# A tile's weight decoding in halves, with its last operation on GpSimd

## The chip, the core and the metric

The kernel runs on one core of a Trainium2 chip. The core has a matrix engine (TensorE, PE in the profile; its weight loads are PEld), a vector engine (VectorE, DVE), an engine for functions of one operand (ScalarE, ACT), a programmable engine (GpSimd, POOL) and one that issues transfers (SyncE, SP). Each engine works through its own instructions in a fixed order, and semaphores make it wait for the others. The metric is the time of one execution on the device in microseconds (us), the median of several runs.

## The reference

The reference computes one attention layer with a memory term and two feed-forward layers behind it, on 2304 rows of 512 numbers:

```python
def _attn_ref(q, k, v, M_prev, z_prev, beta):        # B, H, S, D = 4, 8, 576, 64
    scores = scale * q @ k.T; scores = where(causal, -1e9, scores)
    a = exp(scores - scores.max(-1)); a /= a.sum(-1) + 1e-09
    local = a @ v
    q_p = phi(q)                                      # where(x > 0, x, exp(x) - 1) + 1
    mem_out = (q_p @ M_prev) / (q_p @ z_prev + 1e-06)
    g = sigmoid(beta)
    return g * mem_out + (1 - g) * local

def _moe_ref(x, w_in, w_out):                         # 2304 x 512, 512 x 2048, 2048 x 512
    h = x @ w_in
    return (h * sigmoid(1.702 * h)) @ w_out

def _moe2_ref(x, w_in, w_out):
    h = x @ w_in
    return (h * clip(h + 3, 0, 6) / 6) @ w_out
```

The second layer works on the first one's result. Inputs and outputs are float32.

## The kernel before

The rows are cut into six tiles of 384 (TILES): tiles 0, 1, 3 and 4 are the first 384 rows of a batch, tiles 2 and 5 the last 192 rows of two batches. The hidden width of 2048 is cut into NF = 16 steps f of 128. For a layer, a tile and a step, moe() does the up-projection h (four matmuls, one for each 128 of the 512 inputs, lines 344 to 351), the gate (lines 280 to 301: a function on ScalarE, line 285, then a product on VectorE, line 287, which reads h once more and writes g), and the down-projection y (four accumulating matmuls, lines 317 to 321). In the first layer's first tile the matmuls take float32 operands as they are (lines 346 and 317); everywhere else weights and activations are split in two parts and each product is done as three. Through the first layer h has one buffer, so that the next up-projection can write it only when VectorE has read the last one.

The attention of the later tiles is computed while the earlier ones are in the first layer. Its work for each pair of heads (scores s, line 428; softmax: minimum, exponential, sum and reciprocal, lines 490 to 499; scaling of the probabilities p by GpSimd, line 503; transposes t, line 443; memory term; weighted sum o) is handed out between the matmuls by pump(), and the scheduler described below puts some of it still earlier. The form differs for the last 192 rows of a batch (index 2 and 5): with them come the scalings of p4 and p5, 512 and 64 columns. In the second half of the first tile such work, for the tile with index 2, is what stands between the matmuls.

The weights come from memory as raw 64-bit words seen as pairs of 32-bit words lo and hi, and are decoded in place by conv_w(), one step f at a time: VectorE shifts lo (line 190) and joins it with hi (195); ScalarE brings hi towards a sign (199) while the sign bit of lo is cleared, on ScalarE (201) or on VectorE (203) as ABS says: for the first layer's steps above PRE = 2 on ScalarE where f is even; ScalarE takes the sign of hi (205); VectorE limits lo and multiplies with the sign (210). A step's tile holds the weights of both projections, [128, 2, 512] pairs: index 0 is for the up-, index 1 for the down-projection. For the first layer line 210 writes the result over the raw words, and the first tile's matmuls read it there. The decoding of the 16 steps of the first layer runs during the attention that comes first (steps 0 to 2) and during the first tile.

The kernel is written as generators that hand out instructions in small steps (Chains); what stands in an engine's queue in the end is decided by a scheduler that replays the whole program with its own costs and puts ready instructions in order. A change of one operation can so move others on all engines.

## Time and profile before

| | us |
|---|---|
| median of 3 runs | 1046.57 |
| lowest, highest | 1045.54, 1046.84 |
| profiled execution | 1045.53 |
| its span, first to last instruction | 1043.4 |
| TensorE busy | 1011.2 (97%) |
| VectorE busy | 496.6 (48%) |
| ScalarE busy | 533.1 (51%) |
| GpSimd busy | 295.2 (28%) |

The span is what the views of the trace cover; the rest of an execution's time lies around it. Busy shares are means over the whole program; in the first 260 us, while attention and decoding run, VectorE and ScalarE are busier than later. A wait in a view is the time in which an engine stood idle just before an instruction, with the instruction that let it go.

### The profile page before, as it was taken

What the parts mean: (1) busy time and instruction counts of PE and PEld (TensorE: products, weight loads), DVE (VectorE), ACT (ScalarE), POOL (GpSimd) and SP (SyncE); (2) the same over time, 40 slices, a digit from 0 to 9 for tenths busy, and PEclk for the clock granted to TensorE, in tenths of its full rate; (3) what the DMA queues carried; (4) which work ended last, traced back from release to release, by engine and by line L of the source; (5) the groups of instructions that cost most, each with busy time, mean ns of one, the idle gap of its engine ahead of it and who ended that gap; (6) DMA issues with size and microseconds to landing.
All of it is one profiled execution on the core that took longest, in us unless ns stands there. A gap on an engine that the chain in (4) does not pass through costs nothing.

```text
span 1043.4 us, 15915 instructions
## 1 busy us (share of the span) xinstructions
PE 1011.2 (97%) x5833; PEld 893.5 (86%) x5833; DVE 496.6 (48%) x1209; ACT 533.1 (51%) x1110; POOL 295.2 (28%) x347
## 2 busy tenths in 40 slices
PE   7899999999889899999999999999999999999998
PEld 5555558988777787888889999999999999999998
DVE  6977776665455664534452787871121211211110
ACT  6876755545565565435453787973242332323322
POOL 4422113332233343323232322232222222222221
PEclk9999999999999999999999999999999999999999
DMA  5854324330354445423334475010010010100000
GB/s 188 288 221 141 133 73 149 117 111 27 120 96 95 101 103 110 103 47 91 71 75 160 166 277 180 1 30 31 1 48 15 24 37 1 31 31 1 31 1 31
DMA packets 84829, 92.85 MB, mean 89 GB/s; under 512 B 55056, under 2 KB 64272, under 8 KB 84752
## 3 DMA queue, kind: packets, MB, share of 16 engines
q1 hardware_dynamic: 84752, 91.84, 29.7%
q8 instruction: 46, 0.75, 0.3%
q14 instruction: 31, 0.25, 0.1%
HBM read 61.41 MB, written 9.44 MB: 68 GB/s over the span
## 4 chain that ended last, share of the span: by engine, by line
PE 50%; ACT 5%; DVE 4%; DMA 2%; issue 2%; POOL 0%; ACTq 0%; POOLq 0%; DVEq 0%
PE h L348 8%; PE y L321 8%; PE y L319 8%; PE y L320 8%; PE h L350 8%; PE h L351 8%; DMA xp<-sp 2%; PE o L428 2%; PE s L428 1%; ACT r L199 1%; ACT r L205 1%; DVE w L232 1%; ACT r L201 1%; ACT w L229 1%; DVE wt L210 1%
## 5 line engine op out<-in xcount | busy, mean ns | idle before, releaser
L299 POOL TENSOR_TENSOR g<-t,g 128x384 fp32r<-128x384 f32 x173 | 183.7, 1062 | 493.6 <-ACT g L296 412.8
L348 PE MATMUL h<-xs,w 128*128 128x384 f32 x704 | 241.1, 343 | 8.8 <-DVE t L287 7.6
L350 PE MATMUL h<-xs,w 128*128 128x384 f32 x704 | 236.2, 335 | 0.4 <-DVE w L232 0.3
L319 PE MATMUL y<-g,w 128*128 128x384 f32 x704 | 236.4, 336 | 0.0
L320 PE MATMUL y<-g,w 128*128 128x384 f32 x704 | 236.3, 336 | 0.0
L351 PE MATMUL h<-xs,w 128*128 128x384 f32 x704 | 235.9, 335 | 0.0
L321 PE MATMUL y<-g,w 128*128 128x384 f32 x704 | 224.4, 337 | 0.0
L291 DVE SCALAR_TENSOR_TENSOR t<-t,h 128x384 f32<-128x384 f32 x96 | 53.0, 552 | 278.6 <-ACT t L289 278.5
L348 PEld LDWEIGHTS h<-xs,w 128*128 128x128 f32 x704 | 132.5, 188 | 22.1 <-DVE t L287 9.6
L289 ACT ACTIVATE t<-h,three 128x384 f32<-128x384 f32 x96 | 55.6, 581 | 171.3 <-PE h L351 168.6
L503 POOL TENSOR_SCALAR p<-p,st,omg 128x128 f32<-128x128 f32 (+3 forms) x128 | 88.5, 703 | 172.2 <-DVE st L499 140.8
L321 PEld LDWEIGHTS y<-g,w 128*128 128x128 f32 x704 | 130.4, 188 | 5.6 <-issue 5.0
L296 ACT CAST g<-t 128x384 fp32r<-128x384 f32 x176 | 90.3, 513 | 86.9 <-DVE t L291 49.9
L319 PEld LDWEIGHTS y<-g,w 128*128 128x128 f32 x704 | 132.1, 188 | 2.3 <-issue 1.5
L350 PEld LDWEIGHTS h<-xs,w 128*128 128x128 f32 x704 | 132.5, 188 | 1.1 <-DVE w L232 1.0
L320 PEld LDWEIGHTS y<-g,w 128*128 128x128 f32 x704 | 132.2, 188 | 1.4 <-issue 1.3
L351 PEld LDWEIGHTS h<-xs,w 128*128 128x128 f32 x704 | 132.5, 188 | 0.4 <-DVE xs L277 0.3
L495 ACT ACTIVATE p<-s,st 128x512 f32<-128x512 f32 (+4 forms) x160 | 82.3, 522 | 66.4 <-DVE st L490 64.0
L490 DVE CUSTOM_DVE_ANT_0 s<-s,mask 128x128 f32<-128x128 f32 (+3 forms) x144 | 72.6, 526 | 22.9 <-PE s L428 22.2
L428 PE MATMUL s<-qk 64*128 64x128 f32 (+5 forms) x384 | 70.1, 455 | 8.8 <-ACT p L495 6.1
L285 ACT ACTIVATE t<-h 128x384 f32<-128x384 f32 x96 | 46.9, 489 | 52.6 <-PE h L351 42.7
L287 DVE SCALAR_TENSOR_TENSOR t<-t,h 128x384 f32<-128x384 f32 x80 | 44.0, 551 | 56.8 <-ACT t L285 52.4
(84 smaller groups left out, 1116.2 us busy)
## 6 DMA issues: line engine op xcount, KB each, us to landing
r<-in_w_dram SPq DMA_DIRECT2D x64, 512.0 KB, 6.1
wt<-r SPq DMA_DIRECT2D x32, 256.0 KB, 2.3
vm<-in_vm_dram SPq DMA_DIRECT2D x16, 386.0 KB, 3.5
qk<-in_qk_dram SPq DMA_DIRECT2D x16, 384.0 KB, 3.5
qk<-in_sk_dram SPq DMA_DIRECT2D x32, 192.0 KB, 4.0
x2d<-yo SPq DMA_DIRECT2D x24, 192.0 KB, 2.1
xr<-x2d SPq DMA_DIRECT2D x24, 192.0 KB, 3.0
out_dram<-yo SPq DMA_DIRECT2D x24, 192.0 KB, 1.9
```

Source lines behind the costliest of these rows:

```text
L296: gated["ACT"].append(ACT.copy(out=g[:, 0], in_=t).ins)
L299: d = {"DVE": DVE, "POOL": POOL}[e].tensor_tensor(out=g[:, 1], in0=t, in1=f32(g[:, 0]), op=ALU.subtract)
L319: PE.matmul(ys[d], lhsT=w[:, 0, o:o + 128], rhs=g[:, 0], start=(f == 0), stop=False)
L320: PE.matmul(ys[d], lhsT=w[:, 1, o:o + 128], rhs=g[:, 0], start=False, stop=False)
L321: PE.matmul(ys[d], lhsT=w[:, 0, o:o + 128], rhs=g[:, 1], start=False, stop=(f == NF - 1))
L348: PE.matmul(h, lhsT=w[:, 0, c:c + 128], rhs=x[:, 0], start=first, stop=False)
L350: PE.matmul(h, lhsT=w[:, 1, c:c + 128], rhs=x[:, 0], start=False, stop=False)
L351: PE.matmul(h, lhsT=w[:, 0, c:c + 128], rhs=x[:, 1], start=False, stop=last)
L428: ins = PE.matmul(out, **args).ins
L490: DVE.tensor_tensor_reduce(out=o, in0=o, in1=m, scale=-SCALE, scalar=init, op0=ALU.add, op1=ALU.min, accum_out=out)
L495: return ACT.activation(out=dst, in_=o, func=AF.Exp, scale=-1.0, bias=m, accum_out=s)
L503: (DVE, POOL)[e[norms[0] % len(e)]].tensor_scalar(out=dst, in0=dst, scalar1=s, scalar2=w, op0=ALU.mult, op1=ALU.mult)
```

## The change

For the first layer's steps above 2, the decoding is done in two halves (one per projection), each operation on 512 pairs instead of 1024. The limit and the product with the sign, one operation of VectorE (line 210), become two of GpSimd for each half: a minimum with a constant, in place, and a product of two operands. The sequence within a step is in halves(); each yield hands over to the other chains. Steps 0 to 2 and the second layer are decoded as before.

```diff
+        def signed_aside(to, at):
+
+            POOL.tensor_scalar(out=f32(lo)[:, at], in0=f32(lo)[:, at], scalar1=BIG, scalar2=None, op0=ALU.min)
+            yield
+            POOL.tensor_tensor(out=to, in0=f32(lo)[:, at], in1=f32(hi)[:, at], op=ALU.mult)
+
+        def halves():
+
+            words_of(0)
+            yield
+            bare(0)
+            words_of(1)
+            yield
+            sign(0)
+            bare(1)
+            yield
+            yield from signed_aside(wx[f][:, 0], 0)
+            sign(1)
+            yield
+            yield from signed_aside(wx[f][:, 1], 1)
+
         def chain():
-            first = DVE.tensor_scalar(
-                out=lo, in0=lo, scalar1=29, scalar2=0x40000000, op0=ALU.logical_shift_right, op1=ALU.bitwise_or
-            )
...
+            if layer == 0 and f > PRE:
+                yield from halves()
+                return
+            both = slice(None)
+            words_of(both)
+            yield
+            bare(both)
+            yield
+            sign(both)
             yield
             x = [wx[f]] if layer == 0 else [temp() for _ in range(2)]
             for k, to in enumerate(x):
-                at = slice(None) if layer == 0 else k
-                DVE.scalar_tensor_tensor(
-                    out=to, in0=f32(lo)[:, at], scalar=BIG, in1=f32(hi)[:, at], op0=ALU.min, op1=ALU.mult
-                )
+                signed(to, both if layer == 0 else k)
```

words_of(at) holds the operations of lines 190 and 195 on the part `at`, bare(at) those of 199 and 201 or 203, sign(at) that of 205, signed(to, at) that of 210.

The order of the instructions changes with it from step 3 of the first tile on, on every engine, until well into the second tile; from there TensorE's order is the old one. In the lines of the changed kernel, numbers above the change are 44 higher (L547 is L503 before, L390 is L346, L361 is L317, L331 is L287). Numbers behind a name tell its buffers apart: r12 is the weight tile of step 12, and p4 and p5 the probabilities of the last 192 rows.

GpSimd's queue before, where the first tile reaches steps 9 to 13: only the scalings of the probabilities.

```order
L503 TENSOR_SCALAR p_977<-p_977,st_976,omg_108 128x512
L503 TENSOR_SCALAR p_978<-p_978,st_976,omg_108 128x512
L503 TENSOR_SCALAR p4_1032<-p4_1032,st_976,omp_109 128x512
L503 TENSOR_SCALAR p5_1033<-p5_1033,st_976,omp_109 128x64
L503 TENSOR_SCALAR p_1128<-p_1128,st_1127,omg_108 128x512
L503 TENSOR_SCALAR p_1129<-p_1129,st_1127,omg_108 128x512
L503 TENSOR_SCALAR p4_1184<-p4_1184,st_1127,omp_109 128x512
L503 TENSOR_SCALAR p5_1185<-p5_1185,st_1127,omp_109 128x64
```

GpSimd's queue now, the part that ends with steps 12 and 13 (the scalings of the second pair of heads above are p_1200 to p5_1265 here):

```order
L226 TENSOR_TENSOR r14_1218<-r14_1218 128x512
L547 TENSOR_SCALAR p_1200<-p_1200,st_1199,omg_108 128x512
L547 TENSOR_SCALAR p_1201<-p_1201,st_1199,omg_108 128x512
L226 TENSOR_TENSOR r14_1218<-r14_1218 128x512
L224 TENSOR_SCALAR r12_1101<-r12_1101 128x512 x2
L547 TENSOR_SCALAR p4_1264<-p4_1264,st_1199,omp_109 128x512
L547 TENSOR_SCALAR p5_1265<-p5_1265,st_1199,omp_109 128x64
L226 TENSOR_TENSOR r12_1101<-r12_1101 128x512
L224 TENSOR_SCALAR r13_1168<-r13_1168 128x512
L226 TENSOR_TENSOR r12_1101<-r12_1101 128x512
L224 TENSOR_SCALAR r13_1168<-r13_1168 128x512
L226 TENSOR_TENSOR r13_1168<-r13_1168 128x512
```

The scalings and the decoding now share one queue: the first product of step 12 stands behind the scalings of p4 and p5.

TensorE before, the up-projections of steps 12 (r_1045) and 13 (r_1104), without the number in a name where it can be left out:

```order
L346 MATMUL h<-x_289,r_1045 128x384
L346 MATMUL h<-x_378,r_1045 128x384
L346 MATMUL h<-x_479,r_1045 128x384
L346 MATMUL h<-x_568,r_1045 128x384
L413 MATMUL mem<-vm,phi 128x130 x2
L428 MATMUL s<-qk 128x512 x2
L346 MATMUL h<-x_289,r_1104 128x384
L346 MATMUL h<-x_378,r_1104 128x384
L346 MATMUL h<-x_479,r_1104 128x384
L346 MATMUL h<-x_568,r_1104 128x384
```

TensorE now, the same place, from the memory reads to the up-projection of step 12 (r_1101) and what follows it:

```order
L457 MATMUL mem<-vm,phi 128x130 x2
L472 MATMUL s<-qk 128x512 x2
L487 MATMUL t<-ident,p 128x128 x4
L472 MATMUL o<-ident,mo 128x128 x2
L472 MATMUL o<-pt,vm 64x192 x8
L472 MATMUL o<-t_113,vm 64x64 x2
L390 MATMUL h<-x_289,r_1101 128x384
L390 MATMUL h<-x_378,r_1101 128x384
L390 MATMUL h<-x_479,r_1101 128x384
L390 MATMUL h<-x_568,r_1101 128x384
L472 MATMUL s_1570<-qk 64x512 x2
```

Memory reads, scores, transposes and the weighted sum have moved ahead of step 12's up-projection, and only scores stand between it and step 13's.

VectorE before, up to the gate product of step 12 (g_1222), which frees h for step 13; st holds the softmax's sums:

```order
L203 TENSOR_SCALAR r13_1104<-r13_1104 128x1024
L742 TENSOR_SCALAR mw_1372<-mem_1368 128x4
L743 RECIPROCAL mw_1372<-mw_1372 128x4
L210 SCALAR_TENSOR_TENSOR r13_1104<-r13_1104 128x2x512
L744 TENSOR_TENSOR mw_1372<-mw_1372,gall_107 128x4
L287 SCALAR_TENSOR_TENSOR g_1222<-t_1223,h_1197 128x384
```

VectorE now, up to the same product (g_1306):

```order
L790 TENSOR_TENSOR mo_1475<-mem_1472,mw_1476 128x256
L683 COPY pt_1531<-t_1532 128x4x128
L764 TENSOR_SCALAR phi_1637<-phi_1637 128x192
L542 TENSOR_SCALAR st_1499<-st_1499 128x2
L765 SCALAR_TENSOR_TENSOR phi_1637<-qk_1148,phi_1637 128x192
L543 RECIPROCAL st_1499<-st_1499 128x2
L331 SCALAR_TENSOR_TENSOR g_1306<-t_1307,h_1277 128x384
```

The decoding's last operation is gone from the way of the gate product; softmax work of the scores before step 12 has come ahead of it.

## Rows read from the trace of the kernel before

**Rows 1.** The page's busy time: us, share of the span, instructions of each engine.

```profile
PE 1011.2 (97%) x5833; PEld 893.5 (86%) x5833; DVE 496.6 (48%) x1209; ACT 533.1 (51%) x1110; POOL 295.2 (28%) x347
```

**Rows 2.** Busy time in one stretch: length, the engines, clock, DMA share, GB/s.

```profile
64.30:164.60 100.30, 97.17 (x410) 57.85 (x411) 73.57 (x154) 64.31 (x115) 17.67 (x19) 1.00 0.33 107
```

**Rows 3.** Waits of TensorE from 60 to 165 us: total, times, longest.

```profile
PE h L346 <- DVE g L287: 3.1, 2, 2.5
```

**Rows 4.** Timeline at the longer wait: start, us, instruction, [idle before, releaser].

```profile
136.29 1.20 ACT L205 ACTIVATE r<-r,step_down 128x1024 f32<-128x1024 f32 x1
...
137.53 1.23 DVE L210 SCALAR_TENSOR_TENSOR r<-r 128x1024 f32<-128x1024 f32 x1 [1.23 <-ACT r L205]
138.74 0.55 DVE L287 SCALAR_TENSOR_TENSOR g<-t,h 128x384 f32<-128x384 f32 x1
...
139.34 1.88 PE L346 MATMUL h<-x,r 128*128 128x384 f32 x5 [2.45 <-DVE g L287]
```

**Rows 5.** Timeline between two up-projections, steps 5 and 6.

```profile
85.29 0.49 PE L443 MATMUL t<-ident,p 128*128 128x128 f32 x3
...
86.01 0.55 DVE L287 SCALAR_TENSOR_TENSOR g<-t,h 128x384 f32<-128x384 f32 x1 [1.64 <-ACT t L285]
...
86.62 2.85 PE L346 MATMUL h<-x,r 128*128 128x384 f32 x8
```

**Rows 6.** Durations of operations: ns min/median/max by line, or us in all and mean.

```profile
L190 DVE TENSOR_SCALAR r<-r x16: 673/687/702, 27.5 to 144.6; 128x1024 int32<-128x1024 int32 x16
L195 DVE SCALAR_TENSOR_TENSOR r<-r x16: 1211/1226/1678, 28.3 to 145.3; 128x1024 int32<-128x1024 int32 x16
L210 DVE SCALAR_TENSOR_TENSOR r<-r x16: 1211/1224/1491, 34.4 to 150.0; 128x1024 f32<-128x1024 f32 x16
...
L205 ACT ACTIVATE r<-r,step_down x16: 1197/1240/1313, 31.9 to 148.8; 128x1024 f32<-128x1024 f32 x16
...
L210 DVE SCALAR_TENSOR_TENSOR wt<-r x32: 676/686/1515, 583.9 to 694.6; 128x512 f32<-128x512 f32 x32
...
L229 ACT CAST w<-wt 128x512 fp32r<-128x512 f32 x64 | 36.5, 621 | 16.4 <-DMA wt<-r 10.6 <-DVE wt L210 5.0 <-PE y L317 0.7
...
L503 POOL TENSOR_SCALAR p<-p,st,omg 128x512 f32<-128x512 f32 x32 | 28.5, 900 | 83.7 <-DVE st L499 78.9 <-PE t L443 4.8
...
L299 POOL TENSOR_TENSOR g<-t,g x173: 994/1012/1964, 165.8 to 1033.7; 128x384 fp32r<-128x384 f32 x173
```

**Rows 7.** Timeline of GpSimd's scalings, and VectorE beside the first pair.

```profile
125.19 2.74 POOL L503 TENSOR_SCALAR p<-p,st,omg 128x512 f32<-128x512 f32 x2 [13.09 <-DVE st L499]
125.61 1.68 DVE L195 SCALAR_TENSOR_TENSOR r<-r 128x1024 int32<-128x1024 int32 x1
...
132.83 2.39 POOL L503 TENSOR_SCALAR p<-p,st,omp 128x512 f32<-128x512 f32 x2 [4.90 <-DVE st L499]
...
142.03 1.52 POOL L503 TENSOR_SCALAR p<-p,st,omg 128x512 f32<-128x512 f32 x2 [6.81 <-DVE st L499]
...
158.08 3.05 POOL L503 TENSOR_SCALAR p<-p,st,omp 128x512 f32<-128x512 f32 x2 [14.53 <-DVE st L499]
```

**Rows 8.** Timeline of TensorE alone: scores, up- and down-projections, transposes.

```profile
91.98 1.13 PE L428 MATMUL s<-qk 64*128 64x512 f32 x4
...
127.49 1.19 PE L428 MATMUL s<-qk 64*64 64x512 f32 x8
...
132.48 2.75 PE L346 MATMUL h<-x,r 128*128 128x384 f32 x8
135.67 1.22 PE L428 MATMUL s<-qk 64*128 64x512 f32 x4
...
142.03 2.74 PE L317 MATMUL y<-g,r 128*128 128x384 f32 x8
144.61 0.60 PE L443 MATMUL t<-ident,p 128*128 128x128 f32 x4
...
146.48 1.88 PE L346 MATMUL h<-x,r 128*128 128x384 f32 x5
```

More of the change, by code (lines that the diff above doesn't have):

```diff
@@ L187, in conv_w, with words_of @@
             wx[f] = f32(raw)[:, :, 0:DM]
-        def chain():
+        def words_of(at):
             first = DVE.tensor_scalar(
-                out=lo, in0=lo, scalar1=29, scalar2=0x40000000, op0=ALU.logical_shift_right, op1=ALU.bitwise_or
+                out=lo[:, at], in0=lo[:, at], scalar1=29, scalar2=0x40000000,
+                op0=ALU.logical_shift_right, op1=ALU.bitwise_or,
             )
@@ L195, in chain @@
             DVE.scalar_tensor_tensor(
-                out=lo, in0=hi, scalar=3, in1=lo, op0=ALU.logical_shift_left, op1=ALU.bitwise_xor
-            )
-            yield
-            ACT.activation(out=f32(hi), in_=f32(hi), func=AF.Identity, bias=step_up[:, 0:1])
-            if f % ABS[z][1] < ABS[z][0]:
-                ACT.activation(out=f32(lo), in_=f32(lo), func=AF.Abs)
-            else:
-                DVE.tensor_scalar(out=lo, in0=lo, scalar1=0x7FFFFFFF, scalar2=None, op0=ALU.bitwise_and)
@@ L204, in chain, with bare @@
-            yield
-            ACT.activation(out=f32(hi), in_=f32(hi), func=AF.Sign, bias=step_down[:, 0:1])
+                out=lo[:, at], in0=hi[:, at], scalar=3, in1=lo[:, at],
+                op0=ALU.logical_shift_left, op1=ALU.bitwise_xor,
+            )
+        def bare(at):
+            ACT.activation(out=f32(hi)[:, at], in_=f32(hi)[:, at], func=AF.Identity, bias=step_up[:, 0:1])
+            if f % ABS[z][1] < ABS[z][0]:
+                ACT.activation(out=f32(lo)[:, at], in_=f32(lo)[:, at], func=AF.Abs)
+            else:
+                DVE.tensor_scalar(
+                    out=lo[:, at], in0=lo[:, at], scalar1=0x7FFFFFFF, scalar2=None, op0=ALU.bitwise_and
+                )
@@ new lines, in sign, with signed @@
+        def sign(at):
+            ACT.activation(out=f32(hi)[:, at], in_=f32(hi)[:, at], func=AF.Sign, bias=step_down[:, 0:1])
+        def signed(to, at):
+            DVE.scalar_tensor_tensor(
+                out=to, in0=f32(lo)[:, at], scalar=BIG, in1=f32(hi)[:, at], op0=ALU.min, op1=ALU.mult
+            )
+        def signed_aside(to, at):
+            POOL.tensor_scalar(out=f32(lo)[:, at], in0=f32(lo)[:, at], scalar1=BIG, scalar2=None, op0=ALU.min)
+            yield
+            POOL.tensor_tensor(out=to, in0=f32(lo)[:, at], in1=f32(hi)[:, at], op=ALU.mult)
@@ new lines, in halves, with chain @@
+        def halves():
+            words_of(0)
+            yield
+            bare(0)
[8 more added lines that the diff above has]
+            yield from signed_aside(wx[f][:, 1], 1)
+        def chain():
+            if layer == 0 and f > PRE:
[7 more added lines that the diff above has]
+            sign(both)
```

## The prediction

> **What bounds the kernel now.** I read the page's busy line first [rows 1]: TensorE is busy 97% of a span of 1043.4 us, so it is the bound, and a change elsewhere counts only by the holes in TensorE's row that it opens or closes. Next I cut out the stretch that the change touches. It runs from the first tile's matmuls on step f=3, the first whose weights are decoded the new way, to the last of its 16 steps: 64.30 to 164.60 us. TensorE works 97.17 of those 100.30 us at a granted clock of 1.00 (the upper level, 2.4 GHz), VectorE 73.57, ScalarE 64.31 and GpSimd 17.67 [rows 2]. So 3.1 us is all that this stretch can give, and the waits say who holds it: two waits of the up-projection (h, line 346), both for VectorE's gate product g of line 287 [rows 3]. The timeline at the longer one shows why. The buffer of h is single, so the next up-projection starts when VectorE has read the last one. At 137.53 VectorE stood, in its fixed order, at the decoding's last operation (L210), which had waited 1.23 us for ScalarE's Sign of 136.29; the gate product behind it started only at 138.74, and TensorE lost 2.45 us [rows 4]. That is not the least it can take. At 85.29 the same hand-over (transposes and memory reads between two up-projections, gate product at 86.01, next up-projection at 86.62) cost nothing [rows 5].
>
> I call H(f) and Y(f) the four matmuls of the up- and down-projection of step f; each takes 2.63 us (139.34 to 142.03 to 144.61) [rows 4, 8].
>
> **The change, part by part.** All prices are for one of the 13 steps f=3 to 15, six with the absolute value on ScalarE (even) and seven with it on VectorE.
>
> VectorE loses L210 (1.224 us) and does L190 (0.687) and L195 (1.226) as halves [rows 6]. A two-operand operation of 512 columns takes 0.686 (L210 of the second layer) [rows 6]. The trace has no bit operation of 512; half of 0.687 is the lower end, the whole the upper, and I take 0.45, near the lower, as L195's halves come near half. Even step: 2 x (0.45 + 0.686) = 2.27 instead of 3.14. Odd step: 0.90 instead of 0.69 more. Over 13 steps that is 6 x 0.87 + 7 x 0.66 = 9.8 us less on VectorE. ScalarE's operations of 1.24 become two of about 0.65 (a cast of 512 columns takes 0.621) [rows 6]: some 0.06 more each, about 2 us over the stage, against 36 us in which it is idle [rows 2]. Both lie beside TensorE and cost nothing by themselves.
>
> GpSimd gets 26 minima and 26 products of 512 columns. Minimum: an undisturbed pair of 512 columns took 1.52, so 0.76 each [rows 7]; the mean of all is 0.900 [rows 6]. Product: only 384 columns are in the trace, median 1.012 [rows 6]; that is the lower end, scaled by 512/384 it is 1.35, and I take 1.30. A half is then 2.06, all of them 53.6 us, and GpSimd's load in the stretch becomes 17.7 + 53.6 = 71 of 100 us. No operation of GpSimd on every second word is in the trace; were each twice as long, the load would be 125 us and the stretch some 25 us longer. I hold that unlikely (ScalarE and VectorE read these same words at the speed of dense ones) and keep it outside the range.
>
> GpSimd also scales the attention probabilities (L503), and its queue is in order. Now a decoding product can stand behind a scaling that waits for its softmax, and the other way round; the two order pieces of GpSimd show the first case. The product of step 12 stands behind the scaling p4 and p5, which needs the scores that TensorE does shortly before; behind it queue all of step 13 and the rest of 12, and TensorE waits for these. Does H(12) wait? Its new place: in the kernel before, the work from the scores at 91.98 to 146.48 is 54.5 less the wait 2.45 = 52.05 us, with 14 blocks of 2.63 [rows 4, 8]. The new order has the same attention work before H(12) but 5 blocks fewer, and 4 more products for o (0.6): 39.5 us after these scores. The scores of p4 come 9.3 us ahead of H(12): 5.0 (127.49 to 132.48), then 1.8 for what followed H(12) before, then 2.5 for transposes and o [rows 8]. So they stand at 30.2; their scaling starts 5.3 us later, as 127.49 to 132.83 shows [rows 7, 8], at 35.5; with 1.5 for it and 1.3 for the product the weights are there at 38.3, against 39.5. Up to there GpSimd has 8 halves, two minima, the product and four scalings: 16.5 + 1.5 + 1.3 + 6 = 25.3 us, and from the first scaling (6.4 after its scores, as 135.67 to 142.03) to 39.5 it has 33 [rows 7, 8]. It keeps up, narrowly. I count 0.2 us for H(12), at most 3 if GpSimd's operations take half as long again.
>
> Removed: the two waits of [rows 3]. At both the product stood behind L210, which is no longer on VectorE. Minus 3.1.
>
> Added: the scheduler has put the up-projections closer to each other. Four times now at most about 1.5 us of other work lies between the end of one and the start of the next: before H(8) (scores and transposes), before H(10) (transposes, memory reads, transposes, as in [rows 5]), before H(13) (scores alone) and before the second tile's first one. The hand-over of h through ScalarE and VectorE has to fit in there. Its price is 0 by [rows 5] and 2.45 by [rows 4]; nothing makes one row nearer than the other, since VectorE is lighter but GpSimd now disturbs it, so I take the middle, 1.2, four times: 4.9 us, between 0 and 9.8. At H(13) the gate product now stands behind reciprocals of the softmax (the VectorE pieces), which wait for the exponentials of scores 3.5 us ahead of H(12); by the time H(12) is done these should be there, and behind it only softmax work queues. SP's transfers of wt, qk and vm at the end of the tile change places; each lands under other work, and I count nothing.
>
> Sum: -3.1 + 4.9 + 0.2 = +2.0 us. The profiled execution took 1045.53 us (span 1043.4), 1.04 below the median 1046.57 of the runs; the sum makes it 1047.5, and the median 1048.6.
>
> **Where GpSimd and VectorE meet.** At 125.19 two scalings of 512 columns took 2.74 us instead of 1.52, and L195 at 125.61, which reads two SBUF operands, took 1.68 instead of 1.226 [rows 6, 7]: it reads as if each had waited for the other. The Trainium skill, SBUF — State Buffer, section Who interferes with whom, states this as a rule: GpSimd shares one port pair with VectorE, and an operation of VectorE with two SBUF inputs, or in a two-port mode, and one of GpSimd that reads SBUF exclude each other for the whole instruction, whichever came first. By that rule, which this trace agrees with (2.74 for 1.52), the change puts four more such operations a step on GpSimd while two such halves remain on VectorE.
>
> **Rivals.** (A) The forecast: waits change places, +2.0, from -1 to +5.
> (B) GpSimd and VectorE, excluding each other, become the bound. For: [rows 7]; at 158.08 a pair of 512 and 64 columns took 3.05 us. Booked per step: halves 4.12, scalings 17.67/13 = 1.36, VectorE's two-operand halves 1.37, together 6.85 of the 7.7 us that a step has (100.3/13); if the one-operand ones (two to four of 0.45) count too, 7.75 to 8.65. Against: the halves start early, and only a step's first half must be there for H. From 7.7 booked it decides; 0.6 a step over 13 steps is +8: 1054.6.
> (C) The relief of VectorE decides: the gate product no longer stands behind a wait for Sign, the four close places go as in [rows 5], and 2.6 of the 3.1 us come back: 1044.0. For: 9.8 us less on VectorE. Against: nothing beyond 3.1 is there to gain, and 26 products more hang on an in-order queue.
>
> **The numbers.** A 0.53, B 0.20, C 0.27. What a measurement of this kernel can tell from no change is 0.2%, 2.1 us: 1044.5 to 1048.7. A lies half within it and half above; B is above; of C most is below. Faster 0.25, same 0.33, slower 0.42. A's own range is 1045.5 to 1051.5; for 8 in 10 it must take in most of C and of B: 1043.9 to 1055.
>
> **What would show it.** Right: GpSimd at some 70 us in the stretch, halves near 2.1 to 2.6 us, VectorE without a wait for Sign, the wait of 2.45 gone and waits of 0.5 to 2.5 before H(8), H(10) or H(13); the order of all engines is the same again in the second tile, so the difference must be complete by about 245 us. Wrong: products well over 1.6 us or GpSimd busy without a gap from 100 to 150 us (B), or no hole in TensorE's row over 0.5 us in the stretch (C).

## The result, and the profile after

The changed kernel takes 1059.24 us (median of 4 runs, 1057.71 to 1059.65); the kernel before took 1046.09 on the same chip (4 runs). The ratio is 1.0112, with a 95% interval from 1.0094 to 1.0130: 13 us slower, where 2 were forecast, and above the upper end of the range (1055.0).

The page's busy line of the kernel after, against [rows 1], in the execution that took 1059.07 us (span 1057.3):

```profile
PE 1019.3 (96%) x5833; PEld 898.6 (85%) x5833; DVE 505.5 (48%) x1229; ACT 539.4 (51%) x1142; POOL 363.1 (34%) x399
```

The span grew by 13.9 us. TensorE's busy time grew by 8.1 with the same 5833 matmuls, and what the span holds beside it by 5.8 (1057.3 - 1019.3 = 38.0; before 32.2). So in this sum more than half is no wait: the same matmuls took longer. But more busy time is not yet a loss. Two of the kernels below are as fast as the kernel before, e1 (the halves, all on VectorE) and e4 (no minimum), and in both TensorE is busy for 1016.0 us, 4.8 longer than before. The line of e1:

```profile
PE 1016.0 (97%) x5833; PEld 896.7 (86%) x5833; DVE 499.7 (48%) x1255; ACT 537.6 (52%) x1142; POOL 293.4 (28%) x347
```

Where the loss arises is told by the first eviction of each tile's result on ScalarE (start, us, instruction). After, the end of the first and the second tile:

```profile
177.33 0.86 ACT L415 ACTIVATE yo<-y 128x384 f32<-128x384 f32 x2
...
285.19 0.87 ACT L415 ACTIVATE yo<-y 128x384 f32<-128x384 f32 x2
```

The same two marks before:

```profile
164.22 0.86 ACT L371 ACTIVATE yo<-y 128x384 f32<-128x384 f32 x2
...
272.93 0.87 ACT L371 ACTIVATE yo<-y 128x384 f32<-128x384 f32 x2
```

They are 13.1 and 12.3 us late, and the span ends 13.9 us later: the loss is there when the first tile ends, and stays. One mark alone would not show it, since the scheduler also moves attention work between the tiles: in e14 the first mark, 180.5, is 16 us late and the span ends only 5.1 later. The stretch of step 3 to the last step, against [rows 2] (same columns):

```profile
64.30:177.33 113.03, 102.81 (x423) 60.39 (x422) 83.88 (x184) 72.01 (x149) 84.80 (x72) 0.97 0.29 98
```

It takes 113.0 us instead of 100.3 and holds 13 more matmuls. TensorE is idle for 10.2 us of it, before for 3.1. GpSimd's 17.67 became 84.80. VectorE, from which 13 operations of 1.22 us were taken, went from 73.57 to 83.88, and TensorE's mean clock from 1.00 to 0.97. Groups of instructions by line in the first tile, shapes apart (busy us, mean ns); GpSimd's minimum and product from 43 to 180 us, then VectorE's decoding from 60 to 165:

```profile
L224 POOL TENSOR_SCALAR r<-r 128x512 f32<-128x512 f32 x26 | 42.1, 1625 | 13.1 <-DVE r L208 8.5 <-ACT r L206 3.6 <-ACT r L204 0.6
L226 POOL TENSOR_TENSOR r<-r 128x512 f32<-128x512 f32 x26 | 29.5, 1149 | 0.5
...
L197 DVE SCALAR_TENSOR_TENSOR r<-r 128x512 int32<-128x512 int32 x25 | 24.4, 979 | 0.6
L191 DVE TENSOR_SCALAR r<-r 128x512 int32<-128x512 int32 x25 | 15.2, 609 | 0.0
L208 DVE TENSOR_SCALAR r<-r 128x512 int32<-128x512 int32 x13 | 7.6, 587 | 0.2
```

The minimum takes 1.63 us, not the 0.76 put down for it; the halves are 71.6 us in all, not 53.6. Half of the exclusive-or takes 0.98 instead of about 0.69. VectorE's decoding is 47.2 us here; before, the same window held 44.8, with the limit and the product in it. Nothing of the relief arrived. The same three groups take 35.3 us in e1 below, in halves but without GpSimd's work beside them.

TensorE's waits from 40 to 180 us, against [rows 3] (total, times, longest):

```profile
PE y L361 <- issue: 3.2, 1, 3.2
PE t L487 <- ACT p L539: 2.7, 2, 2.3
PE h L390 <- POOL r L226: 2.1, 3, 0.9
```

"issue" names nobody, so the timeline around the 3.2 us must say it; Y(11) needs the gate product of step 11:

```profile
131.49 0.21 DVE L542 TENSOR_SCALAR st<-st 128x2 f32<-128x2 f32 x1 [2.12 <-ACT p L539]
...
132.26 0.69 DVE L197 SCALAR_TENSOR_TENSOR r<-r 128x512 int32<-128x512 int32 x1
...
132.88 1.27 DVE L191 TENSOR_SCALAR r<-r 128x512 int32<-128x512 int32 x1
132.99 0.76 ACT L204 ACTIVATE r<-r,step_up 128x512 f32<-128x512 f32 x1 [0.88 <-DVE r L197]
...
134.18 1.14 DVE L197 SCALAR_TENSOR_TENSOR r<-r 128x512 int32<-128x512 int32 x1
134.21 0.48 ACT L329 ACTIVATE t<-h 128x384 f32<-128x384 f32 x1
...
135.24 0.54 DVE L331 SCALAR_TENSOR_TENSOR g<-t,h 128x384 f32<-128x384 f32 x1
...
135.88 4.25 PE L361 MATMUL y<-g,r 128*128 128x384 f32 x8 [3.18 <-issue]
```

H(11) was done at about 129.7, but the tanh (L329) stood on ScalarE behind a decoding operation (L204) that waited for VectorE's exclusive-or, and ran at 134.21. The gate product (L331) stood on VectorE behind two more decoding operations, of 1.27 and 1.14 us. These two are the lengthened ones, yet at this place they cost little: the tanh was ready at 134.69, and the gate product began 0.55 us later. The exclusive-or that ScalarE waited for took 0.69, no longer than undisturbed; it was late because it stood behind a softmax sum (L542), for which VectorE had waited 2.12 us on ScalarE's exponential. Most of this hole comes from the fixed order, in which ScalarE and VectorE wait for each other; where they first fell behind lies further ahead and is not traced here. Behind the wait, Y(11) itself took 4.25 us, where such a block takes 2.74 [rows 8]. The windows of 5 us say why (TensorE's clock is the third number from the end). After:

```profile
135.00:140.00 5.00, 4.12 (x9) 2.36 (x10) 3.05 (x10) 3.65 (x9) 5.00 (x5) 0.66 0.15 44
145.00:150.00 5.00, 4.27 (x27) 3.32 (x28) 3.65 (x10) 2.16 (x6) 4.43 (x5) 0.66 0.01 2
285.00:290.00 5.00, 3.54 (x14) 2.92 (x15) 2.44 (x11) 3.38 (x11) 1.00 (x1) 0.55 0.96 311
290.00:295.00 5.00, 5.00 (x22) 4.19 (x21) 1.87 (x9) 2.34 (x9) 1.95 (x4) 0.76 0.40 143
415.00:420.00 5.00, 4.48 (x17) 4.48 (x18) 2.31 (x7) 2.01 (x7) 1.01 (x1) 0.66 0.96 230
```

Before, in the same reading:

```profile
270.00:275.00 5.00, 2.25 (x19) 1.55 (x17) 1.11 (x2) 3.03 (x8) 0.21 (x1) 0.93 0.65 218
275.00:280.00 5.00, 5.00 (x24) 4.15 (x21) 3.06 (x14) 3.48 (x12) 1.22 (x2) 0.73 0.77 243
```

These are all the windows with a lower clock from 30 us to the last 20 us of the span. Five of them after lose at most 5 x (0.34 + 0.34 + 0.45 + 0.24 + 0.34) = 8.6 us at the lower level (1.2 GHz), two before at most 1.7. TensorE was not busy all that time: of 17.1 us at the lower level (135.4 to 138.8, 145.6 to 149.0, 285.5 to 292.4 and 415.3 to 418.7) it worked 15.3, half of which, 7.6 us, the level cost; before, 1.7 (274.3 to 277.7). That is 5.9 of the 8.1 us by which the matmuls got longer. Two of the stretches lie behind the new waits of 3.2 and 2.3 us; the wait of 2.45 us before was followed by none. Nor are the 5.9 us simply a part of the loss: counted the same way, the level costs 6.7 us in e4 (131.7 to 135.2, 275.1 to 281.9 and 312.6 to 316.1), which loses nothing, and 3.3 in e7 (102.1 to 105.6 and 289.9 to 293.4), which loses as much as the changed kernel.

### The profile page after: what moved, and what is told of

Same layout as the page of the kernel before. It is cut to its first block, busy times and chain, and to the rows that moved or that the text cites. A ratio compares the mean times of both kernels' runs of the same rounds, so it can differ in the third digit from the quotient of the medians.

```text
span 1057.3 us, 16067 instructions
## 1 busy us (share of the span) xinstructions
PE 1019.3 (96%) x5833; PEld 898.6 (85%) x5833; DVE 505.5 (48%) x1229; ACT 539.4 (51%) x1142; POOL 363.1 (34%) x399
## 4 chain that ended last, share of the span: by engine, by line
PE 54%; ACT 3%; DVE 2%; DMA 2%; issue 1%; POOL 0%; POOLq 0%; ACTq 0%; DVEq 0%
PE h L392 9%; PE y L365 8%; PE y L363 8%; PE y L364 8%; PE h L394 8%; PE h L395 8%; DMA xp<-sp 2%; PE o L472 2%; PE s L472 1%; ACT r L204 1%; ACT r L214 1%; DVE w L276 0%; DVE wt L218 0%; ACT w L273 0%; POOL p L547 0%
## 5 line engine op out<-in xcount | busy, mean ns | idle before, releaser
L335 DVE SCALAR_TENSOR_TENSOR t<-t,h 128x384 f32<-128x384 f32 x96 | 53.1, 553 | 278.6 <-ACT t L333 278.5
L547 POOL TENSOR_SCALAR p<-p,st,omg 128x128 f32<-128x128 f32 (+3 forms) x128 | 88.8, 705 | 129.4 <-DVE st L543 93.0
L472 PE MATMUL s<-qk 64*128 64x128 f32 (+5 forms) x384 | 71.6, 459 | 8.9 <-ACT p L539 6.1
L329 ACT ACTIVATE t<-h 128x384 f32<-128x384 f32 x96 | 46.9, 490 | 53.2 <-PE h L395 42.2
L331 DVE SCALAR_TENSOR_TENSOR t<-t,h 128x384 f32<-128x384 f32 x80 | 44.1, 551 | 60.8 <-ACT t L329 54.7
```

Of the source, the lines that this page charges most:

```text
L472: ins = PE.matmul(out, **args).ins
L547: (DVE, POOL)[e[norms[0] % len(e)]].tensor_scalar(out=dst, in0=dst, scalar1=s, scalar2=w, op0=ALU.mult, op1=ALU.mult)
```

## The experiments

Theory X: GpSimd's operations lengthen VectorE's, and what stands behind these in the fixed orders gets late. Theory Q: GpSimd's own queue is the bound, since the weights now pass through it. Theory S: the cutting and the new order cost it. Times are medians; each ratio is to the kernel before on the same chip; "halves" is GpSimd's time in the decoding (43 to 180 us or so), "decoding" VectorE's by-line sum from 60 to 165 us.

| run | us | ratio (95%) | halves | decoding |
|---|---|---|---|---|
| changed kernel | 1059.2 | 1.0094 to 1.0130 | 71.6 | 47.2 |
| e1 halves, all on VectorE | 1045.4 | 0.9985 to 1.0006 | 0 | 53.1 |
| e2 whole, on GpSimd | 1052.0 | 1.0045 to 1.0075 | 66.1 | 40.2 |
| e3 minimum written densely | 1059.1 | 1.0114 to 1.0145 | 76.9 | 50.7 |
| e4 no minimum | 1046.4 | 0.9993 to 1.0015 | 28.7 | 40.9 |
| e5 minimum on VectorE | 1052.5 | 1.0036 to 1.0077 | 29.3 | 56.8 |
| e6 GpSimd loaded beside | 1056.7 | 1.0078 to 1.0127 | 74.5 | 66.8 |
| e7 multiplication for minimum | 1059.4 | 1.0102 to 1.0158 | 70.7 | 45.5 |
| e8 odd steps only | 1047.1 | 0.9993 to 1.0018 | 39.7 | 52.0 |
| e10 three steps only | 1046.3 | 0.9976 to 1.0006 | 17.1 | 53.3 |
| e11 minimum by columns | 1053.4 | 1.0049 to 1.0098 | 89.2 | 41.4 |
| e14 absolute values on ScalarE | 1050.3 | 1.0023 to 1.0047 | 71.4 | 37.1 |
| e15 cheap first operation | 1050.8 | 1.0023 to 1.0045 | 47.6 | 42.9 |
| e16 as e14, without GpSimd | 1046.6 | 0.9981 to 1.0001 | 0 | 46.8 |
| e17 no absolute values | 1050.5 | 1.0015 to 1.0035 | 72.6 | 40.2 |

### One part of the change alone: e1, e2

```
e1:  -  yield from signed_aside(wx[f][:, k], k)
     +  yield; signed(wx[f][:, k], k)        # one VectorE operation for a half
e2:  -  yield from halves()
     +  words_of(both); bare(both); sign(both); yield from signed_aside(wx[f], both)
```

> The decoding stays cut into halves of 512 columns, but limit and product are one VectorE operation for each half again, so only the cutting is left of the change. Theory Q (GpSimd's queue: a half costs it 1.59 + 1.06 = 2.65 us there, 69 us for the 26 halves, and the decoding falls behind TensorE): GpSimd is back at about 18 us in the stretch from 64 to 165 us, and the time is near the kernel before, 1045 to 1048 us. Theory X (GpSimd's operations keep VectorE out, its 512-column operations grow from some 0.69 to 0.97 us and what stands behind them gets late): VectorE's operations fall back to 0.69 us or less, the time is 1045 to 1048 us as well. Theory S (the cutting and the new order of the operations cost it): most of the 13 us stays, 1055 us or more. Theory Q and X are not told apart by this run.

> No halves: the decoding operations are 1024 columns wide as in the kernel before, and limit and product are one GpSimd operation each, so only the move to GpSimd is left of the change. Theory Q: the same 5.3 us of GpSimd for each step (minimum about 3.1, product about 2.1), 69 us in all, and a chain that is longer by half a step: 1058 to 1064 us. Theory X: VectorE has 13 fewer operations of 2.4 us but those that are left wait for GpSimd; the loss stays, 1055 to 1062 us. Theory S: with the cutting gone the time is 1045 to 1049 us.

Theory S falls as a cause by itself: the cutting alone costs nothing (e1). The move alone (e2) costs 6 us, half of the loss, with 66.1 us of GpSimd time instead of 71.6 (13 minima of 3.01 us, 13 products of 2.07); all three ranges missed it. (The 2.4 us that its expectation gives for VectorE's operation are 1.22 [rows 6].) So the loss comes with GpSimd's load, and in halves the load does more harm. Why it does is not shown; VectorE's operations of 1024 columns number half as many.

### The minimum: e3, e7, e4, e15

```
e3:  out = 512 dense words of the step before, instead of f32(lo)[:, at]
e7:  -  scalar1=BIG, scalar2=None, op0=min      +  scalar1=1.0, scalar2=None, op0=mult
e4:  -  POOL.tensor_scalar(... op0=min)
e15: -  scalar1=BIG, scalar2=None, op0=min      +  scalar1=1.0, scalar2=1.0, op0=mult, op1=mult
```

> As the changed kernel, but the minimum reads its half in strides and writes it densely into words that the step before has left free, and the product reads it there. Theory Q: what made the minimum cost 1.59 us is that it both reads and writes every second word; it falls towards the 0.76 us of the dense scalings (0.8 to 1.1), GpSimd has 10 to 20 us less in the stretch, and the time falls by half the loss or more, 1046 to 1053 us. Theory X with a cause that does not depend on the minimum's length (each start of an operation of one engine waits for the other's): VectorE's 512-column operations stay near 0.97 us and the time stays above 1054 us. If the minimum keeps 1.5 us or more, strides in its output are not its price, and the time is that of the changed kernel.

> As the changed kernel, but GpSimd's first operation multiplies by 1.0 where it took the minimum with the limit (the limit is left out, a part of the computation); width, strides and waits are the same. If the operation is the price, it falls from 1.59 to 0.75 to 1.0 us, GpSimd has 26 x 1.85 = 48 us of halves, and the time is 1046 to 1050 us. If reading every second word is the price, it stays at 1.55 us or more and the time stays near 1059 us.

> As the changed kernel without the minimum (the limit on the decoded value is left out, a part of the computation); GpSimd has the 26 products alone. Theory Q: 26 times 1.06 = 27.6 us of GpSimd, with its scalings about 45 us of the 100, nothing late: 1043 to 1048 us, and what is left over the kernel before is the price of the move itself. Theory X: if the two-input product alone keeps VectorE out, its 512-column operations stay near 0.9 us and the time stays above 1052 us; if it is the minimum that does, they fall to about 0.69 us and the time is as by Q.

> As the changed kernel, but GpSimd's first operation multiplies by 1.0 twice, which took 0.71 us alone where the minimum took 1.60 (the limit is left out, a part of the computation): the price that the prediction had put for the minimum (0.76 us). If that price was the term that failed, the time is what the prediction gave, 1046 to 1051 us; if it stays above 1055 us, the price of the minimum was not the cause.

A dense destination changes nothing (1.57 us each), nor does a multiplication in place of the minimum (1.65). Without the minimum the loss is gone; with a first operation of 0.73 us, close to the price that the prediction had put, the time is 1050.8 us, inside its range, and 3.7 of the 13 us are left. The minimum's price is the term that was mis-sized. (e4, e7 and e15 leave the limit out, a part of the computation.) What makes it long is neither the words it reads nor the operation, and both guesses on that were wrong; the two kernels of prices settle it.

### The prices: e9, e12

> None of the computation: in stretches of their own, one after the other, GpSimd runs six operations of 512 columns of one kind, VectorE eight, first each engine alone and then both at once, on tiles of their own. GpSimd's kinds: the minimum with every second word as source and as destination, only one of them, neither; a scaling by two columns (the attention's form), dense and in strides; the product of strided and of dense sources. VectorE's: the shift-and-exclusive-or with two strided sources, the shift with one, the gate's form with one source in PSUM, a product. Theory X: VectorE's operations with all operands in SBUF grow beside GpSimd's, the one with two sources most (0.69 to 1 us or more), while the gate's form keeps its 0.55 us, as it did in all kernels so far. Theory Q needs no growth. On the minimum: if reading in strides is its price, strided-to-strided and strided-to-dense take 1.5 us and dense-to-dense 0.8 or less, and the strided scaling costs twice the dense one; if it is the form with one constant, all four take 1.5 us.

> None of the computation: six GpSimd operations of 512 strided columns in each stretch: the minimum with one constant, with two operations and two constants, with one column, with two operations and two columns; the multiplication with two constants, with one column, with two columns. If the second operation makes the fast form, all with two take 0.9 us and all with one 1.55; if the column does, those with columns take 0.9 us. At the end the fast minimum beside VectorE's shift and exclusive-or: these grow to 0.8 to 1.0 us if the two engines keep each other out, as beside the scaling.

Timeline of e9: GpSimd alone, six operations each: the minimum with one constant, strided and dense; the scaling by two columns, dense; the product; and the product beside the exclusive-or. Then VectorE, eight operations each: exclusive-or, shift and gate form alone; all three beside the minimum; all three beside the product. Each was measured in one execution.

```profile
7.67 9.59 POOL L149 TENSOR_SCALAR A<-A 128x512 f32<-128x512 f32 x6 [7.25 <-ACT A L144]
...
19.08 9.32 POOL L152 TENSOR_SCALAR A<-A 128x512 f32<-128x512 f32 x6 [1.82 <-ACT A L144]
...
52.52 5.13 POOL L161 TENSOR_SCALAR A<-A,C 128x512 f32<-128x512 f32 x6 [1.90 <-issue]
...
66.98 6.63 POOL L167 TENSOR_TENSOR A<-A 128x512 f32<-128x512 f32 x6 [2.35 <-ACT V L146]
...
157.78 8.80 POOL L167 TENSOR_TENSOR A<-A 128x512 f32<-128x512 f32 x6 [2.35 <-ACT V L146]
...
85.31 5.78 DVE L173 SCALAR_TENSOR_TENSOR V<-V 128x512 int32<-128x512 int32 x8 [79.37 <-ACT V L146]
92.55 3.67 DVE L176 TENSOR_SCALAR V<-V 128x512 int32<-128x512 int32 x8 [1.45 <-ACT V L144]
97.95 4.68 DVE L179 SCALAR_TENSOR_TENSOR G<-T,P 128x384 f32<-128x384 f32 x8 [1.73 <-ACT T L144]
110.63 6.72 DVE L173 SCALAR_TENSOR_TENSOR V<-V 128x512 int32<-128x512 int32 x8 [1.68 <-ACT V L146]
122.21 6.78 DVE L176 TENSOR_SCALAR V<-V 128x512 int32<-128x512 int32 x8 [4.86 <-ACT V L144]
134.13 4.67 DVE L179 SCALAR_TENSOR_TENSOR G<-T,P 128x384 f32<-128x384 f32 x8 [5.14 <-ACT T L144]
157.75 10.09 DVE L173 SCALAR_TENSOR_TENSOR V<-V 128x512 int32<-128x512 int32 x8 [5.32 <-ACT V L146]
169.30 7.97 DVE L176 TENSOR_SCALAR V<-V 128x512 int32<-128x512 int32 x8 [1.45 <-ACT V L144]
178.99 4.67 DVE L179 SCALAR_TENSOR_TENSOR G<-T,P 128x384 f32<-128x384 f32 x8 [1.73 <-ACT T L144]
```

Strides are not the price (1.60 against 1.55 us each), the form is: the scaling takes 0.86, the product 1.11. VectorE's shift grows from 0.46 to 0.85 us beside the minimum and 1.00 beside the product; the exclusive-or from 0.72 to 0.84 and 1.26. The gate form, one of whose sources is in PSUM, keeps 0.58 beside either. It was expected that the operation with two sources grows most; it does not: beside the minimum the shift gains 0.39 us and the exclusive-or 0.12. So X's lengthening is there, by itself, without any dependence between the two engines.

Timeline of e12, GpSimd, six of each on strided columns: the minimum with two operations and two constants, with one column, with two operations and two columns; the multiplication with two constants.

```profile
19.05 12.16 POOL L161 TENSOR_SCALAR A<-A 128x512 f32<-128x512 f32 x6 [1.79 <-ACT A L144]
33.02 10.07 POOL L164 TENSOR_SCALAR A<-A,C 128x512 f32<-128x512 f32 x6 [1.80 <-issue]
44.91 13.14 POOL L167 TENSOR_SCALAR A<-A,C 128x512 f32<-128x512 f32 x6 [1.82 <-ACT A L144]
59.85 4.25 POOL L170 TENSOR_SCALAR A<-A 128x512 f32<-128x512 f32 x6 [1.80 <-ACT A L144]
```

Both guesses of e12 missed: neither the second operation nor the column makes it fast. Of the forms measured only "multiply, then multiply" is (0.71 with constants, 0.87 with columns); one operation, minimum or multiplication, takes 1.6 to 1.7, two minima 2.0 to 2.2. Beside two minima by columns the shift took 0.72 us and the exclusive-or 0.86.

### Which engine is late: e6, e14, e16, e17

```
e6:  e1, and beside each half on words that nobody reads
     +  POOL.tensor_scalar(out=a, in0=a, scalar1=BIG, scalar2=None, op0=min)
     +  POOL.tensor_tensor(out=a, in0=a, in1=b, op=mult)
e14: -  ABS = ((0, 1), (1, 2), (1, 1))     +  ABS = ((0, 1), (1, 1), (1, 1))
e16: e1 with the line of e14
e17: -  else: DVE.tensor_scalar(... bitwise_and)     (the steps 3 to 15)
```

> The kernel with halves whose limit and product stay on VectorE (1045.4 us), and beside each half GpSimd runs a minimum and a product of the same 512 columns on words that the step before has left free; nothing waits for them but GpSimd's own queue. So GpSimd is as loaded as in the changed kernel, and the decoding does not pass through it. Theory Q (the decoding waits in GpSimd's queue): TensorE's waits stay small, and the time is 1045 to 1049 us. Theory X (GpSimd's minimum keeps VectorE out): VectorE's 512-column operations, the 26 of limit and product among them, grow to 0.9 us or more, it has some 60 us of decoding in the 100, the steps of the first tile get late, and the time is 1053 to 1060 us.

> As the changed kernel, but all the absolute values are ScalarE's; VectorE is lighter by 14 operations of 0.58 us (8 us) and ScalarE has as many more of about 0.6 us. Theory X: part of the loss comes back, 1050 to 1056 us, unless ScalarE becomes late in its place. Theory Q: no change or worse, 1058 to 1063 us.

> Halves with limit and product on VectorE (1045.4 us), and all the absolute values on ScalarE as in the run that got 9 us back. If that gain was VectorE's relief beside GpSimd, there is nothing to gain here: 1045 to 1048 us. If the move of the absolute values gains in any kernel, 1036 to 1042 us.

> As the changed kernel, without VectorE's absolute values (the odd steps 3 to 15 leave out a part of the computation; 14 operations of 0.58 us); GpSimd and ScalarE are as loaded as before. Theory X: 1047 to 1053 us, as with the absolute values on ScalarE or better. Theory Q: 1056 us or more, since GpSimd's 70 us of halves are still there.

In e6 no weight passes through GpSimd, and 10 of the 13 us are there. Its trace is of an execution of 1060.2 us, 3.5 above its median. VectorE's decoding there (limit and product, exclusive-or, shift, absolute value):

```profile
L220 DVE SCALAR_TENSOR_TENSOR r<-r 128x512 f32<-128x512 f32 x26 | 20.8, 802 | 6.3 <-ACT r L216 6.1
L199 DVE SCALAR_TENSOR_TENSOR r<-r 128x512 int32<-128x512 int32 x25 | 19.9, 794 | 0.4
L193 DVE TENSOR_SCALAR r<-r 128x512 int32<-128x512 int32 x25 | 16.0, 639 | 0.0
L210 DVE TENSOR_SCALAR r<-r 128x512 int32<-128x512 int32 x14 | 10.1, 720 | 0.1
```

The same four groups in e1, without GpSimd beside them:

```profile
L197 DVE SCALAR_TENSOR_TENSOR r<-r 128x512 int32<-128x512 int32 x25 | 18.8, 752 | 0.4
L218 DVE SCALAR_TENSOR_TENSOR r<-r 128x512 f32<-128x512 f32 x26 | 17.8, 689 | 7.4 <-ACT r L214 7.2
L191 DVE TENSOR_SCALAR r<-r 128x512 int32<-128x512 int32 x24 | 10.5, 438 | 0.0
...
L208 DVE TENSOR_SCALAR r<-r 128x512 int32<-128x512 int32 x13 | 6.0, 458 | 0.1
```

66.8 us against 53.1, and TensorE's long waits in e6 are for VectorE (total, times, longest):

```profile
PE h L403 <- DVE r L220: 3.8, 1, 3.8
PE h L403 <- DVE g L344: 3.7, 4, 1.6
```

A third long wait, 2.6 us, is for ScalarE; none of TensorE or VectorE is for GpSimd. So X is enough for a loss of this size. The reverse points the same way. Taking the absolute values, some 8 us, off VectorE gives some 9 us back, whether ScalarE does them (e14) or nobody (e17), with GpSimd as busy as in the changed kernel, and without GpSimd the same move gives nothing (e16: 1046.6). But the absolute value also stands ahead of GpSimd's minimum (8.5 us of GpSimd's idle time in the changed kernel end with L208), so what earlier minima gave is not separated from it. Theory Q isn't needed for most of the loss, and yet it is there: in the changed kernel three waits, 2.1 us, end with GpSimd's product, and in e7, which loses as much, three waits of Y:

```profile
PE y L361 <- POOL r L224: 2.9, 2, 2.2
PE y L361 <- POOL r L226: 2.7, 1, 2.7
```

In e3 they are four, 4.8 us. So GpSimd's load reaches TensorE by both ways, and by which one more depends on the order of the build. In e14 and e17 3 to 4 us stay, with waits of TensorE for GpSimd's products and for scalings behind them (e14 4.7 us, e17 3.1).

### From which load on: e8, e10, e5, e11

```
e8:  if f % 2: limit and product on GpSimd, else on VectorE      e10: if f in (4, 7, 10)
e5:  DVE.tensor_scalar(... op0=min), POOL.tensor_tensor(... op=mult)
e11: scalar1=big[:, 0:1], scalar2=big[:, 0:1], op0=min, op1=min
```

> As the changed kernel, but only the odd steps (3, 5, ... 15) take limit and product to GpSimd: 14 halves for it instead of 26, 37 us, with its scalings 55 us of the 100; the even steps leave them on VectorE. Theory Q (capacity of GpSimd's queue): with half of its time free nothing gets late, 1045 to 1049 us, and the loss per half is not constant. Theory X (each of GpSimd's minimums costs VectorE its time): the loss goes by the number of halves, 14 / 26 of 13 us, 1051 to 1055 us.

> As the changed kernel, but only the steps 4, 7 and 10 take limit and product to GpSimd, 6 halves of 26; the other steps' halves leave them on VectorE. By both theories nothing gets late through six halves, 1044 to 1048 us. Whether a little relief of VectorE ahead of the twelfth step pays is what it tells: if TensorE's wait there (2.5 us in the kernel before) goes, 1043 to 1045 us; if not, 1046 us as before.

> As the changed kernel, with the minimum on VectorE (one operation of 512 columns for each half, about 0.42 us undisturbed) and the product alone on GpSimd. By both theories the minimum on GpSimd is what costs, and the time is 1045 to 1048 us; above 1052 us the two operations in place of one, or the way over a second engine, would be the price, and not the minimum's length.

> As the changed kernel, but the minimum is written as the attention's scaling is: two operations (minimum and minimum again), the limit from a column of 128 values instead of a constant. The kernel that measures prices showed 1.5 to 1.6 us for the form with one constant, strided or dense, and 0.86 us for the form with two columns. If the form is the price: 0.85 to 1.1 us each, GpSimd 26 x (0.9 + 1.1) = 52 us of halves and some 70 in the stretch, and the time falls to 1046 to 1051 us; VectorE's operations still grow beside it (0.72 to 0.84 us and more). If a minimum costs 1.55 us in any form, the time stays near 1059 us.

14 halves on GpSimd cost nothing, as Q expected, 26 cost 13 us: the loss is no price per half, against X in its plain form. There is room in the first tile. Between the two lies e15, with 47.6 us of GpSimd's time and 3.7 of loss. Relief for VectorE ahead of the wait of 2.45 us, which is before H(13), pays nothing either (e10), and no version here beats the kernel before. e5 missed its expectation: with the minimum on VectorE its decoding rises to 56.8 us, and TensorE waits 3.6 us once for a softmax's exponential, with a mean clock of 0.83 from 130 to 150 us. By that expectation's own rule the minimum's length on GpSimd is then not the only price: the same work added to VectorE costs 6 us. e11 was to shorten the minimum and lengthened it to 2.29 us; GpSimd then worked without a gap from 65 to 150 us, and yet the kernel lost 7 us, not 13. Neither Q nor X by itself explains that.

### Two that tell nothing apart: e13, e18

```
e13: words_of: +  if layer == 0 and f > PRE: return      (ahead of the exclusive-or)
e18: words_of: +  if layer == 0 and f > 7: return
```

> As the changed kernel, but the steps 3 to 15 leave out VectorE's shift-and-exclusive-or (a part of the computation); GpSimd's minimum and product stay, some 2.65 us for each of 26 halves. VectorE is lighter by 26 operations of 0.97 us, 25 us. Theory X (VectorE is late because GpSimd keeps it out): VectorE has time to spare, and the time falls to 1045 to 1050 us with GpSimd as busy as before. Theory Q (GpSimd's queue is the bound whatever VectorE does): GpSimd needs its 70 us of halves and 18 of scalings as before, and the time stays at 1054 us or more.

> As the changed kernel, but the steps 8 to 15 leave out VectorE's shift-and-exclusive-or (a part of the computation; 16 operations of 0.97 us, 15 us of VectorE's time); GpSimd is as loaded as before. Theory X: the waits of the changed kernel at 136 and 146 us (3.2 and 2.3 us, and the lower clock behind them) go, 1045 to 1052 us. Theory Q: TensorE waits there for GpSimd's product instead, 1056 us or more.

They took 1059.1 (ratio 1.0093 to 1.0138) and 1063.7 us (1.0133 to 1.0164), the opposite of what X says. Most of their long waits come early. In e13 TensorE's longest wait, 6.1 us for the exponential of a softmax, ends at 68.1 us, ahead of most halves; from 43 to 65 us ScalarE was busy 21.8 of 22 us, and after 79 us no wait is over 1.4 us. In e18 three of the four longest waits lie before 100 us, and from 65 to 100 ScalarE worked 29.4 of 35 us. Without the exclusive-or the build puts the decoding of later steps earlier into ScalarE's order, and softmax and tanh stand behind it. That another place became late is how the traces read; no run tests it. What X or Q would cost with a free VectorE stays open.

## Why the prediction was wrong

The bound and the place were right: TensorE bounds, and the waits arise in the first tile. That the difference would be complete by 245 us is nearly so: 12.3 of the 13.9 us are there at 285. Of the four small waits that it foresaw, those before H(8), H(10) and the second tile's first up-projection came, with 0.7 to 0.8 us each, and the one before H(13) was 0.1: 2.2 us where the sum had 4.9. The old wait of 2.45 us, which also stood before H(13), is gone, and H(12), for which 0.2 was counted, did not wait. What the sum had at nothing came instead: 0.5 to 0.9 us before H(5), H(6) and H(7), and the two large holes, 3.2 us before Y(11) and 2.3 before a transposition. Three of the small waits, before H(6), H(7) and H(8), end with GpSimd's product and not with the gate product. Four steps failed; the first is the term that was mis-sized.

- The price of the minimum, 0.76 us, was taken from the scaling: "an undisturbed pair of 512 columns took 1.52" [rows 7]. Both are one-source operations of GpSimd, but the scaling is the one fast form measured; the minimum takes 1.60 alone and 1.63 here. The product was near (1.15 for 1.30). A half is 2.77 us instead of 2.06. That the strided operation might cost twice was priced (125 us of load) and left out as unlikely; strides were rightly dismissed, but the factor of two came by another way. With an operation of the foreseen price (e15) the kernel takes 1050.8 us, within the range: 3.7 more than before, where the sum had 2.0.
- "9.8 us less on VectorE" did not come. From 60 to 165 us it would have left 44.8 - 9.8 = 35.0 us of decoding. The cutting was priced rightly (the same groups take 35.3 in e1), but beside GpSimd they take 47.2. The prediction priced the halves as undisturbed, and told of the two engines' meeting [rows 7] only beside the sum and in rival B. It had to be a term of the sum, since most of VectorE's decoding now lies beside a busy GpSimd.
- Rival B was given 0.20, and its own condition decides against that chance: it counted 6.85 us booked of 7.7 a step, "From 7.7 booked it decides". With the measured half it is 5.54 + 1.36 + 1.37 = 8.3, which by B's own sum, 0.6 a step, gives its 1054.6. B is the nearest of the three to what happened, but 4.6 us short, and not by its full exclusion, which e9 does not show: what gets late is the chain through VectorE and ScalarE, and GpSimd's queue with it.
- The clock had no term. The holes that ended at 136 and 146 us were followed by the lower level, and matmuls at 1.2 GHz cost 5.9 us more than before. How much of that is loss stays open, as e4 and e7 show.

The Trainium skill, SBUF — State Buffer, section Who interferes with whom, on which rival B leaned, says that the engine which comes second is fully blocked, and that a VectorE instruction with one SBUF source outside the two-port modes does not contend. The second half agrees with e9 (the gate form: 4.68 us alone, 4.67 beside the product). The shift, with one SBUF source as well, does get longer there (3.67 to 7.97); no run shows in which mode it works, so it doesn't test that half. The first is too hard for the exclusive-or: eight of them and six products take 5.78 + 6.63 = 12.41 us one after the other, and 10.09 together. And by the Trainium skill, GPSIMD Engine Reference, section 4.1 Engine selection, GpSimd runs one-source elementwise work at roughly line rate and two-source work at half of VectorE's speed; here the one-source minimum (1.60 us) is slower than the two-source product (1.11), so the measurement decides.

What stays open: the size of the loss for a given load (e11 loses half of what e7 does with more GpSimd time, e2 with some 5 us less), how it divides between late VectorE work and GpSimd's own queue, and the free-VectorE case. The orders differ between these builds; no run held the order fixed.

## What to carry to other kernels

An operation moved to GpSimd must be priced by its own form, alone and beside the VectorE work that it will meet, before its load is added up; and the work left on VectorE is re-priced too: here 16 us were taken away, and what was left grew by 18, 6.5 of them by the cutting and 12 beside GpSimd. Look at whether anything waits for the relieved engine at all: with the limit left out altogether and only the product moved, nothing was gained (e4). Here, where all queues are in order, 14 halves were free and 26 cost 13 us. And don't read TensorE's busy time or its clock as a loss before a run of the same time has been compared: e1 and e4 have 4.8 us more of the one, e4 pays 5 us more for the lower level, and neither loses anything.

## What the hardware showed

- GpSimd, 512 columns of f32 (e9, e12): multiply-multiply 0.71 us with constants, 0.87 with columns; one minimum or one multiplication 1.6 to 1.7; two minima 2.0 to 2.2; the strided product 1.11. A stride of two words hardly matters (1.60 against 1.55).
- Beside GpSimd's product, VectorE's shift of one SBUF source takes 1.00 us for 0.46, more than beside the slower minimum (0.85); for the gate form, with a source in PSUM, nothing changes (0.58, e9).
- GpSimd's work on words that nobody waits for made VectorE's decoding 66.8 us instead of 53.1 and the kernel 10 us slower (e6).
